# Retention and a Mish feed-forward layer on one core: state copies on one engine, one load and four scalings moved, four transposes moved

## The chip, the cores and the metric

The kernel runs on one core of a Trainium2 chip. The metric is device time in microseconds (us) of one execution, as the median of several runs. A core has five engines with a queue of instructions each, which run in the order in which they were issued: TensorE (PE in the profile: matmuls and transposes, with its weight loads as PEld), VectorE (DVE), ScalarE (ACT), GpSimd (POOL) and SyncE (SP). Transfers are issued from the queues of SyncE, ScalarE and GpSimd. The engines meet only through semaphores. In this kernel matmuls write to PSUM, a memory cut into banks, from which VectorE and ScalarE read; GpSimd works on the other on-chip memory, SBUF.

## What is computed

```python
def _attn_ref(q, k, v):                      # q, k, v: 8 batches, 8 heads, 576 positions, 64
    scores = scale * np.matmul(q, k.transpose(0, 1, 3, 2))
    gamma = 1.0 - 2.0 ** (-5.0 - np.arange(H))
    rel = pos[:, None] - pos[None, :]
    Dmat = np.where(rel >= 0, gamma[:, None, None] ** rel[None, :, :], 0.0)
    return np.matmul(scores * Dmat[None], v)

def _moe_ref(x, w_in, w_out):                # x: 4608 x 512, w_in: 512 x 2048, w_out: 2048 x 512
    h = x @ w_in
    g = h * np.tanh(log1p(exp(h)))           # Mish
    return g @ w_out
```

Inputs and the output are float32. The decay factorises: gamma^(i-j) = gamma^i * gamma^-j, so the kernel scales q by `gq` and v by `gv`, and only the diagonal blocks need a mask.

## The kernel before

**Chunks and states.** The 576 positions of a batch are cut into four chunks of 128 and one of 64; the last chunks of two neighbouring batches share one chunk of 128 rows. That gives 36 chunks: numbers 0 to 7 are the first chunks of the eight batches, and then come the others in pairs of batches (8 to 14 for batches 0 and 1, 15 to 21 for batches 2 and 3, and so on). The first chunks need no earlier state and go through functions of their own (`f_...`). Every other chunk needs the *state* of its batch, the sum of k times v over all earlier chunks. `state(upto)` adds one chunk to the running sum in a PSUM bank (`st`, one buffer; eight matmuls, L336) and copies the sum to SBUF (`ssb`) in two halves, each multiplied by a column of `diag` that is 1 for one half of the partitions and 0 for the other: ScalarE makes the first half (L339), VectorE the second (L340). Both read the same bank and the next `state` writes to it. The first term of a batch's state takes k from `k0[b]` (`load_k0`, L252, a transfer on GpSimd's queue) and v from `v0s[b]` (`f_state`, L248, a product on GpSimd).

**Steps of a chunk n.** `load(n)` issues q, k and v on GpSimd's queue (L266, L270). P: VectorE scales q (L276). V: GpSimd scales v (L282). T: eight transposes on TensorE into a buffer of the PSUM pool `sc` (two buffers) and a ScalarE copy (L291, L292) for n < 18, a transposing transfer on SyncE's queue for the others (L294). S: scores (L304) into a buffer of `sc`, and the masked copy by VectorE (L308). O: state and masked scores to the chunk's result (L354, L359) into the same buffer, and VectorE's copy to `xT` (L363).

**Tiles.** Four chunks make a tile t of 512 rows (t = 0 to 8). For a tile `g1(t, f)` computes one of 16 slices of the first projection (four matmuls, L373, then Mish on ScalarE, L375), and `g2(t, i)` a quarter of the second projection of one chunk (four matmuls, L388). After the last quarter `stores()` copies the sums by VectorE (L424) and issues the output's transfer; the copy frees the PSUM bank (`ops` with one buffer, or `hp` with two).

**Order.** The order is written out by hand, and each engine's queue follows it. After the first stage (chunks 0 to 7) comes a loop over 24 steps u = 4j + w (L511 to L540) in which tile 1 is projected while chunks 8 to 13 are prepared. In it GpSimd's queue gets, at w = 0 of j = 1 to 4: V of chunk 8 + j, `f_state(1, j - 1)` (batches 4 to 7) and `load(11 + j)`, and at j = 5: V of chunk 13, the loads of chunks 16 and 17, `load_k0(2)` and `load_k0(3)`. The state of batch 2 begins in the next loop, at t = 2, i = 4. That loop (L543 to L577) runs over t = 2 to 9 and 16 steps i, where w = i % 8: scores stand at w = 0, outputs at w = 4, with up to one state at w = 0 and two at w = 4 (before and after the outputs). `by_pe` is true only in the tile at t = 2; there the transposes of chunks n + 2 and n + 3 stand at w = 6 and 7.

The pool `vraw` has eight buffers, which hold the values of the eight first chunks and then those of the later chunks.

Of the kernel before, what the change touches and what calls it, by code (L numbers as in the profile page):

```python
# [12 lines left out]
AX = mybir.ActivationFunctionType  # L13
OP = mybir.AluOpType
# [3 lines left out]
def kernel(  # L18
# [18 lines left out]
    nc = tc.nc  # L37
    B, H, S, D = q.shape
    assert (B, H, S, D) == (8, 8, 576, 64)
    P = 128  # L40
    NP = H // 2
# [28 lines left out]
    op = ctx.enter_context(tc.tile_pool(name="op", bufs=4))  # L70
# [25 lines left out]
    v0 = {}  # L96
# [55 lines left out]
    gv = consts.tile([P, 5, H], F32)  # L152
# [4 lines left out]
    diag = consts.tile([P, 2], F32)  # L157
# [21 lines left out]
    v0s = {}  # L179
# [61 lines left out]
                                 start=(p == 0), stop=True, skip_group_check=True)  # L241
        copy(xts[t][:, :, ts(b, P)], ot)

    def f_state(t, b):

        n = 4 * t + b
        v0s[n] = first.tile([P, H, D], BF16, name="v0s", bufs=B)
        nc.gpsimd.tensor_tensor(v0s[n], v0[n], gv[:, 0, :].unsqueeze(2).to_broadcast([P, H, D]), op=OP.mult)  # L248

    def load_k0(b):  # L250
        k0[b] = first.tile([P, H, D], BF16, name="k0", bufs=B)
        nc.gpsimd.dma_start(out=k0[b], in_=k[b, :, 0:P, :].rearrange("h p d -> p h d"))  # L252
# [3 lines left out]
    def load(n):  # L256
        if n >= n_chunks:
            return
        b, c = chunks[n]
        qr = io.tile([P, H, D], F32, name="qraw")  # L260
        vr = io.tile([P, H, D], F32, name="vraw", bufs=8)
        qks = io.tile([P, 2, H, D], BF16, name="qks", bufs=9)
        live[n] = {"q": qr, "v": vr, "qks": qks}
        for t, src in ((qr, q), (qks[:, 1], k), (vr, v)):
            if c < 4:
                nc.gpsimd.dma_start(  # L266
                    out=t, in_=src[b, :, ds(P * c, P), :].rearrange("h p d -> p h d"))
            else:
                for e in range(2):
                    nc.gpsimd.dma_start(  # L270
                        out=t[ds(64 * e, 64)],
                        in_=src[b + e, :, ds(512, 64), :].rearrange("h p d -> p h d"))
# [49 lines left out]
    def state(upto):  # L322

        if upto >= n_chunks or done[0] > state_of[upto]:
            return False
        b, c = states[done[0]]
        done[0] += 1
        if c == 0:
            ks, vs = k0[b], v0s[b]
            st_ps[b] = ps_st.tile([P, NP, 64], F32, name="st")  # L330
        else:
            ks, vs = live[index[b, c]]["qks"][:, 1], live[index[b, c]]["vs"]
        st = st_ps[b]
        for p in range(NP):
            for e in range(2):
                nc.tensor.matmul(st[ds(64 * e, 64), p, :], lhsT=ks[:, 2 * p + e, :], rhs=vs[:, 2 * p + e, :],  # L336
                                 start=(c == 0 and p == 0), stop=True, skip_group_check=True)
        ssb = tr.tile([P, 2, NP, 64], BF16, name="ssb", bufs=6)
        nc.scalar.activation(ssb[:, 0], st, AX.Copy, scale=diag[:, 0:1])  # L339
        nc.vector.tensor_scalar(ssb[:, 1], st, diag[:, 1:2], None, op0=OP.mult)  # L340
        st_sb[b, c] = ssb
        return True

# [24 lines left out]
    def g1(t, f):  # L368
        if f == 0:
            gts[t] = gp.tile([P, nF, NCH * P], BF16, name="gT")  # L370
        hp = ps_h.tile([P, NCH * P], F32, name="hp")
        for c in range(KC):
            nc.tensor.matmul(hp, lhsT=w_in_t[:, c, ts(f, P)], rhs=xts[t][:, c, :],  # L373
                             start=(c == 0), stop=(c == KC - 1))
        nc.scalar.activation(gts[t][:, f, :], hp, AX.Mish)  # L375

    def g2(t, i):
        s, part = divmod(i, 4)
        if t == nT - 1:
            s = (s + 3) % 4  # L380
        if part == 0:
            if (t == nT - 1 and s % 2) or (t == 1 and s < 2):
                outs[t] = ps_h.tile([P, d_model], F32, name="hp")
            else:
                outs[t] = ps_o.tile([P, d_model], F32, name="ops")
        ops = outs[t]
        for f in range(4 * part, 4 * part + 4):
            nc.tensor.matmul(ops, lhsT=gts[t][:, f, ts(s, P)], rhs=w_out_t[:, f, :],  # L388
                             start=(f == 0), stop=(f == nF - 1))
        if part == 3:  # L390
            ready.append((t, s, ops))
# [3 lines left out]
    def stores():  # L395
        while ready:
            store(*ready.pop(), nc.vector.tensor_copy)
# [24 lines left out]
    def store(t, s, ops, copy):  # L422
        ot = op.tile([P, d_model], F32, name="res")
        copy(ot, ops)  # L424
        b, c = chunks[NCH * t + s]
        if c < 4:
            nc.sync.dma_start(out=out[ds(b * S + P * c, P), :], in_=ot)
        else:
            for e in range(2):
                nc.sync.dma_start(out=out[ds((b + e) * S + 512, 64), :], in_=ot[ds(64 * e, 64), :])  # L430

    def att(n, steps):
        if n >= n_chunks:
            return
        for step in steps:
            {"P": step_p, "V": step_v, "T": step_t, "S": step_s, "O": step_o}[step](n)
# [10 lines left out]
    for step in "T0 W2 S0 W1 T1 T2 S1 T3 S2 S3".split():  # L447
        n = int(step[1])
# [23 lines left out]
    for b in range(4):  # L472
        f_state(0, b)
        load(N0 + b)
# [9 lines left out]
    for i in range(nF):  # L484
        for step in steps.get(i, "").split():
            n = int(step[1])
# [15 lines left out]
    def more_loads(upto):  # L502
        for _ in range(2):
            if queued[0] <= upto:
                load(queued[0])
                queued[0] += 1
# [4 lines left out]
    for u in range(24):  # L511
        j, w = divmod(u, 4)
        if w == 0 and j > 0:
            att(N0 + j, "PV")
            if j < 5:
                f_state(1, j - 1)
                load(N0 + j + 3)
            else:
                more_loads(N0 + j + PF)
                load_k0(2)  # L520
                load_k0(3)
        elif w == 1 and j > 0:
            if j > 3:
                state(N0 + j - 1)
            if j < 5:
                att(N0 + j - 1, "S")
            if j < 4:
                state(N0 + j - 1)
            if j > 1:
                att(N0 + j - 2, "O")  # L530
            if j == 4:
                state(N0 + j - 1)
            stores()
        elif (w == 3 and j < 5) or (w == 2 and j == 5):
            att(N0 + j, "T")
        stores()
        if u < nF:
            g1(1, u)
        else:
            g2(1, u - nF)  # L540


    for t in range(2, nT + 1):  # L543
        for i in range(nF):
            n, w = NCH * (t + 1) + i // 8 * 2, i % 8
            if t in (3, 4) and i in (4, 12):
                load_k0(2 * t - 2 + i // 8)
            by_pe = n + 2 < NPE
            if w == 0:
                state(n + 1)  # L550
                stores()
                att(n, "S")
                att(n + 1, "S")
            if w == 4:
                state(n + 3)
                stores()
                att(n, "O")
                att(n + 1, "O")
                state(n + 3)
            if by_pe and w in (1, 3):  # L560
                att(n + 2 + w // 2, "P")
            if w in (0, 1):
                att(n + 2 + w, "V")
                more_loads(n + 2 + w + PF)
            if w - (6 if by_pe else 0) in (0, 1):
                att(n + 2 + w % 2, "T")
            if w == 7 and n + 4 >= NPE:
                att(n + 4, "P")
                att(n + 5, "P")
            stores()  # L570
            if t < nT:
                g1(t, i)
            if t == 2:
                if i % 2:
                    g2(1, 8 + i // 2)
            elif t < nT or i < 12:
                g2(t - 1, i)  # L577
# [32 lines left out]
```

## Time and profile before

| | |
|---|---|
| median of 3 runs | 326.68 us (324.84 to 327.05) |
| profiled execution | 327.7 us, of it 326.0 us span |
| TensorE busy | 304.8 us (93% of the span) |
| VectorE, ScalarE, GpSimd busy | 126.5, 128.4, 142.9 us |
| mean granted TensorE clock | 0.99 |
| two halves of the state copy, each x32 | ScalarE 473 ns, VectorE 480 ns |
| `f_state` on GpSimd, x8 | 1053 to 1530 ns, median 1090 |
| q scaling on VectorE (L276), x28 | 678 to 1416 ns, median 684 |
| `load_k0`, x8, from issue to landing | 7.4 to 16.3 us, median 8.8 |

The page gives busy times and groups of instructions with a mean duration of one; the answers of the trace give instructions in order of time (start, duration, engine, line, operation, output <- inputs, with the idle time of the engine before and what ended it in square brackets), and sums of waits (total, number, longest). In the page's rows of 40 digits each digit is a slice of the span and gives a busy share in tenths, or the clock that TensorE was granted.

### The profile page before, as it was taken

What the parts mean: (1) busy time and instruction counts of PE and PEld (TensorE: products, weight loads), DVE (VectorE), ACT (ScalarE), POOL (GpSimd) and SP (SyncE); (2) the same over time, 40 slices, a digit from 0 to 9 for tenths busy, and PEclk for the clock granted to TensorE, in tenths of its full rate; (3) what the DMA queues carried; (4) which work ended last, traced back from release to release, by engine and by line L of the source; (5) the groups of instructions that cost most, each with busy time, mean ns of one, the idle gap of its engine ahead of it and who ended that gap; (6) DMA issues with size and microseconds to landing.
All of it is one profiled execution on the core that took longest, in us unless ns stands there. A gap on an engine that the chain in (4) does not pass through costs nothing.

```text
span 326.0 us, 5926 instructions
## 1 busy us (share of the span) xinstructions
PE 304.8 (93%) x2439; PEld 151.6 (46%) x2478; DVE 126.5 (39%) x195; ACT 128.4 (39%) x223; POOL 142.9 (44%) x174
## 2 busy tenths in 40 slices
PE   5889999999939999999999999999999999999995
PEld 2543445555415545444544444545454444444444
DVE  2722555655623634443434443434344332000111
ACT  4666237773415453342424333333343332333200
POOL 5572359999992894819280808062010000000000
PEclk9999999999969999999999999999999999999999
DMA  7999999977999599999999969981322300010031
GB/s 177 214 205 244 238 223 258 216 126 149 208 188 151 91 199 135 227 126 167 141 182 114 194 112 169 123 161 53 60 68 56 77 32 34 32 32 32 34 96 65
DMA packets 79850, 44.10 MB, mean 135 GB/s; under 512 B 63056, under 2 KB 71504, under 8 KB 79824
## 3 DMA queue, kind: packets, MB, share of 16 engines
q0 software_dynamic: 47376, 24.98, 53.3%
q1 hardware_dynamic: 31872, 18.23, 26.1%
q10 hardware_dynamic: 576, 0.52, 0.6%
q8 instruction: 19, 0.31, 0.4%
q14 instruction: 7, 0.06, 0.1%
HBM read 38.80 MB, written 9.44 MB: 148 GB/s over the span
## 4 chain that ended last, share of the span: by engine, by line
PE 71%; DMA 11%; POOL 7%; issue 4%; DVE 3%; ACT 2%; SPq 1%; ACTq 0%; DVEq 0%; POOLq 0%
PE hp L373 29%; PE ops L388 25%; PE hp L388 4%; DMA w_in_t<-in_moe_w_in_dram 4%; DMA k<-in_k_dram 2%; PE hp L405 2%; PE st L336 2%; POOL vs L282 2%; DMA vraw<-in_v_dram 2%; ACT ssb L339 2%; DMA gT<-in_k_dram 2%; DMA qks<-in_k_dram 2%; PE sc L304 1%; POOL qraw L266 1%; DVE ssb L340 1%
## 5 line engine op out<-in xcount | busy, mean ns | idle before, releaser
L373 PE MATMUL hp<-xT,w_in_t 128*128 128x512 bf16 x548 | 142.4, 383 | 3.0 <-DVE gq L475 0.8
L375 ACT ACTIVATE gT<-hp 128x512 bf16<-128x512 f32 x144 | 86.1, 598 | 129.3 <-PE hp L373 117.3
L388 PE MATMUL ops<-w_out_t,gT 128*128 128x512 bf16 x429 | 110.0, 379 | 1.0 <-DVE res L424 0.5
L373 PEld LDWEIGHTS <-w_in_t 128*128 128x128 bf16 x576 | 53.9, 98 | 64.7 <-DMA w_in_t<-in_moe_w_in_dram 2.4
L388 PEld LDWEIGHTS <-gT 128*128 128x128 bf16 x496 | 48.3, 98 | 59.4 <-issue 2.8
L424 DVE COPY res<-ops 128x512 f32<-128x512 f32 x28 | 19.2, 687 | 75.2 <-PE ops L388 74.9
L340 DVE TENSOR_SCALAR ssb<-st,diag 128x256 bf16<-128x256 f32 x32 | 15.4, 480 | 75.4 <-ACT ssb L339 75.4
L266 POOL DMA_DIRECT2D qraw<-in_q_dram x24 | 22.5, 938 | 39.9 <-DVE qks L276 36.9
L282 POOL TENSOR_TENSOR vs<-vraw,gv 128x512 bf16<-128x512 f32 x28 | 30.2, 1087 | 20.8 <-issue 14.2
L308 DVE TENSOR_TENSOR sm<-sc,mask 128x1024 bf16<-128x1024 f32 x28 | 33.0, 1216 | 6.0 <-PE sc L304 6.0
L339 ACT ACTIVATE ssb<-st,diag 128x256 bf16<-128x256 f32 x32 | 15.1, 473 | 26.5 <-PE st L336 26.5
L266 POOL DMA_DIRECT2D vraw<-in_v_dram x24 | 21.9, 911 | 2.3 <-DMA w_out_t<-in_moe_w_out_dram 2.0
L266 POOL DMA_DIRECT2D qks<-in_k_dram x24 | 21.7, 906 | 2.4 <-DMA w_out_t<-in_moe_w_out_dram 2.4
L276 DVE TENSOR_TENSOR qks<-qraw,gq 128x512 bf16<-128x512 f32 x28 | 21.7, 806 | 1.2 <-DMA qraw<-in_q_dram 1.2
L363 DVE CAST xT<-sc 128x512 bf16<-128x512 f32 x24 | 15.3, 681 | 0.0
L388 PE MATMUL hp<-w_out_t,gT 128*128 128x512 bf16 x61 | 14.6, 379 | 0.3 <-issue 0.2
L270 POOL DMA_DIRECT2D qraw<-in_q_dram x8 | 5.6, 708 | 15.7 <-DVE qks L276 15.7
L292 ACT COPY qkT<-sc 128x1024 bf16<-128x1024 bf16 x10 | 10.1, 1012 | 4.7 <-PE sc L291 4.7
L248 POOL TENSOR_TENSOR v0s<-vraw,gv 128x512 bf16<-128x512 f32 x8 | 9.9, 1240 | 0.0
L354 PE MATMUL sc<-qkT,ssb 128*64 128x128 bf16 (+1 forms) x224 | 9.5, 213 | 0.0
L336 PEld LDWEIGHTS <-qks 128*64 128x64 bf16 x192 | 5.1, 110 | 9.3 <-issue 7.6
L359 PE MATMUL sc<-sm,vs 128*64 128x128 bf16 x192 | 9.4, 219 | 0.0
(93 smaller groups left out, 202.5 us busy)
## 6 DMA issues: line engine op xcount, KB each, us to landing
out_dram<-res SPq DMA_DIRECT2D x31, 256.0 KB, 2.3
vraw<-in_v_dram POOLq DMA_DIRECT2D x28, 256.0 KB, 6.8
qraw<-in_q_dram POOLq DMA_DIRECT2D x24, 256.0 KB, 5.1
qks<-in_k_dram POOLq DMA_DIRECT2D x24, 128.0 KB, 5.7
w_in_t<-in_moe_w_in_dram POOLq DMA_DIRECT2D x4, 512.0 KB, 8.4
w_out_t<-in_moe_w_out_dram POOLq DMA_DIRECT2D x4, 512.0 KB, 22.3
gT<-in_q_dram SPq DMA_DIRECT2D x15, 128.0 KB, 6.1
gT<-in_k_dram SPq DMA_DIRECT2D x9, 128.0 KB, 9.0
```

The source lines that it names most:

```text
L266: nc.gpsimd.dma_start(out=t, in_=src[b, :, ds(P * c, P), :].rearrange("h p d -> p h d"))
L276: nc.vector.tensor_tensor(live[n]["qks"][:, 0], live[n]["q"], gq[:, c, :].unsqueeze(2).to_broadcast([P, H, D]), op=OP.mult)
L282: nc.gpsimd.tensor_tensor(vs, live[n]["v"], gv[:, c, :].unsqueeze(2).to_broadcast([P, H, D]), op=OP.mult)
L308: nc.vector.tensor_tensor(sm.rearrange("p e n i -> p (e n) i"), sc.rearrange("p e n i -> p (e n) i"), m.unsqueeze(1).to_broadcast([P, 2 * ...
L336: nc.tensor.matmul(st[ds(64 * e, 64), p, :], lhsT=ks[:, 2 * p + e, :], rhs=vs[:, 2 * p + e, :], start=(c == 0 and p == 0), stop=True, skip ...
L339: nc.scalar.activation(ssb[:, 0], st, AX.Copy, scale=diag[:, 0:1])
L340: nc.vector.tensor_scalar(ssb[:, 1], st, diag[:, 1:2], None, op0=OP.mult)
L363: nc.vector.tensor_copy(xts[t][:, :, ts(s, P)], ot)
L373: nc.tensor.matmul(hp, lhsT=w_in_t[:, c, ts(f, P)], rhs=xts[t][:, c, :], start=(c == 0), stop=(c == KC - 1))
L375: nc.scalar.activation(gts[t][:, f, :], hp, AX.Mish)
L388: nc.tensor.matmul(ops, lhsT=gts[t][:, f, ts(s, P)], rhs=w_out_t[:, f, :], start=(f == 0), stop=(f == nF - 1))
L424: copy(ot, ops)
```

## The change

The state copy becomes one VectorE instruction: `st` is read twice by a repeated dimension and multiplied by the two columns of `diag`, repeated along the row. `f_state` takes its engine as an argument; the calls for batches 4 to 7 now go to VectorE, and stand at w = 2 instead of w = 0. `load_k0(2)` moves from j = 5 (behind the loads of chunks 16 and 17) to j = 4 (ahead of the load of chunk 15). In the main loop the stores at w = 0 go ahead of the state, and TensorE's transposes at t = 2 move from w = 6 and 7 to w = 5 and 6.

```diff
-    def f_state(t, b):
+    def f_state(t, b, engine=nc.gpsimd):
 
         n = 4 * t + b
         v0s[n] = first.tile([P, H, D], BF16, name="v0s", bufs=B)
-        nc.gpsimd.tensor_tensor(v0s[n], v0[n], gv[:, 0, :].unsqueeze(2).to_broadcast([P, H, D]), op=OP.mult)
+        engine.tensor_tensor(v0s[n], v0[n], gv[:, 0, :].unsqueeze(2).to_broadcast([P, H, D]), op=OP.mult)
...
         ssb = tr.tile([P, 2, NP, 64], BF16, name="ssb", bufs=6)
-        nc.scalar.activation(ssb[:, 0], st, AX.Copy, scale=diag[:, 0:1])
-        nc.vector.tensor_scalar(ssb[:, 1], st, diag[:, 1:2], None, op0=OP.mult)
+        nc.vector.tensor_tensor(
+            ssb.rearrange("p e n d -> p e (n d)"),
+            st.rearrange("p n d -> p (n d)").unsqueeze(1).to_broadcast([P, 2, NP * 64]),
+            diag.unsqueeze(2).to_broadcast([P, 2, NP * 64]), op=OP.mult)
...
         if w == 0 and j > 0:
             att(N0 + j, "PV")
             if j < 5:
-                f_state(1, j - 1)
+                if j == 4:
+                    load_k0(2)
                 load(N0 + j + 3)
             else:
                 more_loads(N0 + j + PF)
-                load_k0(2)
                 load_k0(3)
...
             stores()
+        elif w == 2 and 0 < j < 5:
+            f_state(1, j - 1, nc.vector)
         elif (w == 3 and j < 5) or (w == 2 and j == 5):
             att(N0 + j, "T")
...
             if w == 0:
+                stores()
                 state(n + 1)
-                stores()
                 att(n, "S")
                 att(n + 1, "S")
...
-            if w - (6 if by_pe else 0) in (0, 1):
-                att(n + 2 + w % 2, "T")
+            if w - (5 if by_pe else 0) in (0, 1):
+                att(n + 2 + (w == 1 or w == 6), "T")
```

## The prediction

> **What bounds the kernel now.** I read the page's busy times and clock row first, then TensorE's waits by length, then the stretch with the longest of them in order of time, then one steady tile in order of time.
>
> On the page, in 40 slices of 8.15 us:
>
> ```profile
> PE   5889999999939999999999999999999999999995
> PEclk9999999999969999999999999999999999999999
> ```
>
> TensorE is the bound: 304.8 us busy of a span of 326.0. Nothing off it counts unless TensorE waits for it. One slice stands out, the 12th, with a third of the work, and the granted clock falls in it. The waits of TensorE:
>
> ```profile
> PE st L336 <- DMA k<-in_k_dram: 5.6, 2, 5.3
> ...
> PE st L336 <- DVE ssb L340: 2.3, 10, 0.3
> ```
>
> The first is one wait of 5.3 us (the second of its two is 0.3, at 142.67, of the same length and in the same place as the ssb waits, so I count it with them). In order of time, around it:
>
> ```profile
> 87.27 1.82 POOL L252 DMA_DIRECT2D k<-in_k_dram  x2
> ...
> 89.08 0.39 PE L359 MATMUL sc<-sm,vs 128*64 128x128 bf16 x8
> ...
> 94.77 0.43 PE L336 MATMUL st<-v0s,k 128*64 128x64 bf16 x8 [5.30 <-DMA k<-in_k_dram]
> ```
>
> Batch 2's k is issued at 87.27 and lands 7.4 us later, while TensorE wants it at 89.4. GpSimd issues it late because its queue has no gap from 49.5 to 100. A steady tile in order of time, with both kinds of small wait (start, duration, engine, line):
>
> ```profile
> 183.28 1.04 PE L373 MATMUL hp<-xT,w_in_t 128*128 128x512 bf16 x3
> ...
> 183.74 0.68 DVE L424 COPY res<-ops 128x512 f32<-128x512 f32 x1
> ...
> 184.48 1.02 PE L388 MATMUL ops<-w_out_t,gT 128*128 128x512 bf16 x4 [0.16 <-DVE res L424]
> ...
> 190.61 0.32 PE L336 MATMUL st<-vs,qks 128*64 128x64 bf16 x8
> ...
> 190.97 0.47 ACT L339 ACTIVATE ssb<-st,diag 128x256 bf16<-128x256 f32 x1 [0.52 <-PE st L336]
> ...
> 191.48 0.48 DVE L340 TENSOR_SCALAR ssb<-st,diag 128x256 bf16<-128x256 f32 x1 [4.79 <-ACT ssb L339]
> ...
> 192.11 0.32 PE L336 MATMUL st<-vs,qks 128*64 128x64 bf16 x8 [0.28 <-DVE ssb L340]
> ```
>
> The two halves of the state copy run one after the other, and the second state's matmuls wait for both because they write the bank that is being read. At 184.48 the second projection waits for the output copy, which was queued behind the state copy.
>
> **Part 1: k of batch 2 sooner, four scalings off GpSimd.** The four v0s products at L248 hold GpSimd's queue 1.48 + 1.47 + 1.47 + 0.99 = 5.4 us (start to next start at 60.34, 65.52, 70.69, 77.29). Without the first three, the scaling of chunk 12's v ends at 77.29 - 4.42 = 72.9, and k is issued there: 14.4 us sooner. L252's transfers took 7.4 to 16.3 us to land (median 8.8), so it lands at about 81.7, at worst 89.2. TensorE wants it at 89.4, less some 0.6 that parts 2 and 3 save before it (0.25 at 73.76, 0.34 at 83.85): 88.8. Cover 7.1 us; at the worst landing 0.4 us would remain. k is moved past chunk 15's three loads and those of chunks 16 and 17; chunk 15's are put back by 0.9 us (one issue) but are 4.4 sooner by the scalings, the others run 5.4 sooner.
>
> What the hole costs is read against the next block of the same kind, at i = 12 of this tile. There the second state starts 1.50 us after the first (108.89 to 110.39), so here it would have at 88.26 + 1.50 = 89.76 instead of 94.77: 5.0 us. From that state to the next scores it takes 6.43 us there (to 116.82) and 8.29 here (to 103.06): 1.9 us, the lower clock (granted 0.50 in 92 to 96, 0.66 in 96 to 100). **Gain 6.9 us.** What is late next: the following inputs are values of chunk 15 (wanted by the state at 108.89, in the new time near 101.5, and scaled at 95.36 - 5.4 = 90.0) and q of chunk 18 (loading once chunk 13's q is freed). GpSimd then waits for freed q buffers again, as it does at 107.01 now (6.88 us), so TensorE sets its pace.
>
> The v0s products on VectorE: the same form at L276 takes 0.68 alone and 1.21 to 1.42 beside GpSimd products (59.76, 64.87, 69.90). VectorE idles 1.77, 1.63 and 1.91 us in each pass of this stage (before 62.74, 67.77, 73.22). It gets 0.7 to 1.5 more, and 0.2 for the longer copy. Queued behind it is the next chunk's q scaling, which ended at 66.14 for transposes at 70.09: 4 us of room. I take nothing; if the cover is gone, each pass is late by 0.1. The Trainium skill (GPSIMD Engine Reference, Specifications) says that GpSimd shares its SBUF interfaces with VectorE and collides with instructions that have two SBUF inputs, which speaks against this move; its rule would put every one of the four at the contended price, 4 x 0.74 = 3.0 us more VectorE time in all, still under the idle time. One new wait: loads of chunks 12 to 15 may take over the value buffers that these products read. GpSimd reaches the values of 13, 14, 15 near 65.8, 70.5, 75.5 and the products end near 65.8, 70.8, 76.4: up to 0.9 us of GpSimd's queue (with the next k and loads behind it), inside the 7.1.
>
> **Part 2: the state copy in one instruction.** No row shows this form. Nearest: L363, 512 elements from PSUM, 0.68; L308, a product with a broadcast from PSUM, 1.22 for 1024, which at L363's slope gives the same 0.68. Upper end: twice L340's 0.48, 0.96. I take 0.68, by the row of equal size. From the first state's start it is ready after 0.36 (190.61 to 190.97) + 0.68 + about 0.12 (191.96 to 192.11, and 0.06 at 73.76) = 1.16; TensorE is ready itself after 1.05 to 1.1 (the same outputs without a state, 272.59 to 273.64: 1.05). Second states now start 1.40 (five) or 1.50 (six) after the first: 11 x 1.45 - 11 x 1.16 = 3.2, and 0.3 for the one in the hole, less 0.1 for rounding: **3.4 us**. At 0.96 the sum is 1.44 and the gain 0.1. The Trainium skill (VectorE: DVE Perf Modes, the perf-mode tier table) gives a product no more than one element a cycle from PSUM and a single-source operation up to two, against merging the copies; by its formula of (N + 151) cycles at 0.96 GHz a 512-element product would be an estimated 0.69 us, which leaves the gain at 3.3. ScalarE loses 15.1 us of copies; TensorE never waits for it in the steady tiles, so nothing.
>
> **Part 3: the output copy before the state copy.** It matters only where a state stands at w = 0: 83.85, 135.04, 184.48, 250.14. Four matmuls at 0.216 from 183.28 end at 184.14; the next start at 184.48: 0.34 lost, the same at the others. Put first, the copy starts when its sums are done (182.4) and ends at 183.1. The state copy waits up to 0.7 for it, with scores' masks behind, needed only four steps later (6 us). **Gain 4 x 0.34 = 1.4 us.**
>
> **Part 4: transposes a step sooner.** Only in the tile at t = 2, four of them. They write score buffers that the xT copies free: at 0.36 + 0.68 + 0.62 = 1.7 us after the first state, against transposes at 1.1 + 0.24 + 0.86 = 2.2 (outputs, second state, one projection slice): no wait, 0.5 to spare. They may free ScalarE before the scores: scores to first projection take 0.78 at 103.06 and 116.82 against 0.55 at 149.93. Bounds +0.5 and -0.5; I take 0.
>
> **Sum.** 6.9 + 3.4 + 1.4 = 11.7 us. The profiled execution took 327.7 (span 326.0, 1.7 around it), 1.0 above the median 326.68. Profiled 316.0, span 314.3; median **315.0 us**.
>
> **Rivals.** A: the hole goes, but the copy costs 0.96 and the transposes nothing: 6.9 + 1.4 = 8.3, 318.4 us. For it: an unseen form. Against: two rows at 0.68. B: another input takes the hole's place (a transfer that lands 16 us late, a buffer wait) and half of it stays, 3.4 of 6.9: 318.4 with part 2, 321.6 without. Against: GpSimd is 5 us ahead everywhere. C: the change moves k, but TensorE's stop hangs on something else issued in the same place, and only small gains come: about 323.5, no difference. Against: it restarts 7.4 us after this issue, the shortest landing of L252. D, slower: the product with two broadcast operands is slow out of PSUM, in the twelve places where a second state waits. The present chain equals a product of 0.99; to eat the 8.3 us of the other parts it must take 0.99 + 8.3 / 12 = 1.68 us, and 2.0 gives about 330.5. For it: both operands repeat elements, which no PSUM row does. Against: the longest PSUM row is 1.22, for twice the columns.
>
> **How the numbers follow.** A measurement can tell about 1% from no change, here 323.4 and 329.9. Chances: forecast 0.60 (313 to 317.5, by the landing and 0.5 of part 4), A 0.17, B 0.10, C 0.07, D 0.06. Faster: forecast, A and B, 0.87; same C, 0.07; slower D, 0.06. The range 312.5 to 320.5 takes in the forecast, A and a part of B.
>
> **What would show it.** The 12th slice at 9 in both rows; no wait of L336 for k over 0.5; one VectorE copy of about 0.68 with 32 of it and no L339; second states 1.15 after first; no wait for L424 at w = 0. Wrong if a wait over 2 us stands between 80 and 110, if the copy takes over 1 us, or if VectorE's lateness shows as TensorE waits between 60 and 80.

## The result and the profile after

The changed kernel takes 314.94 us in the median (314.66 to 315.26, four runs) against 325.76 (322.56 to 327.05, four runs) before: a ratio of 0.968 with a 95% interval of 0.961 to 0.976. The forecast was 315.0. The profiled execution took 315.04 us, 313.3 of it span, against 327.7 and 326.0. An execution more than 1.5% above the fastest of its kernel counts as slow and is left out of the medians and ratios here.

The same two rows of the page, TensorE's busy tenths and its granted clock in 40 slices of 7.83 us:

```profile
PE   5889999999999999999999999999999999999995
PEclk9999999999999999999999999999999999999999
```

The slice with a third of the work is gone, and so is the lower clock. The longest of TensorE's waits in the changed kernel, by total, number and longest (L375, L390 and L426 are now the lines of the first projection, the second projection and the output copy):

```profile
PE hp L200 <- DVE qb L188: 2.6, 1, 2.6
PE ops L174 <- DVE lnd L129: 1.3, 1, 1.3
PE hp L375 <- DMA w_in_t<-in_moe_w_in_dram: 0.8, 1, 0.8
```

None is for k, for a state copy or for an output copy; what is left stands before 20 us, apart from three of 0.2. The place of the hole, in order of time:

```profile
72.62 0.93 POOL L252 DMA_DIRECT2D k<-in_k_dram  x1
...
86.84 0.32 PE L336 MATMUL st<-vs,qks 128*64 128x64 bf16 x8
...
87.94 0.32 PE L336 MATMUL st<-v0s,k 128*64 128x64 bf16 x8
...
94.37 0.62 PE L304 MATMUL sc<-qkT 64*128 64x128 bf16 x16
```

Batch 2's k is issued at 72.62 instead of 87.27 and landed 3.9 us later, 11.4 us ahead of its use. The second state follows the first after 1.10 us, where it took 6.51, and the next scores follow that state after 6.43, where they took 8.29. The steady tile, at the same steps as the one shown of before:

```profile
171.97 0.32 PE L336 MATMUL st<-v0s,k 128*64 128x64 bf16 x8
172.08 0.69 DVE L426 COPY res<-ops 128x512 f32<-128x512 f32 x1 [3.92 <-PE ops L390]
...
172.69 0.68 DVE L339 TENSOR_TENSOR ssb<-st,diag 128x512 bf16<-128x512 f32 x1
172.77 1.04 PE L375 MATMUL hp<-xT,w_in_t 128*128 128x512 bf16 x3
...
173.64 1.03 PE L390 MATMUL ops<-w_out_t,gT 128*128 128x512 bf16 x4
```

The output copy now goes ahead of the state copy (172.69) and ends at 172.77, so the second projection follows the first without a gap. The new state copy takes 674 to 693 ns (median 683, 32 of them).

Where the 12.7 us between the two spans come from, read as distances between the same instructions in both traces:

| stretch | before | after | difference |
|---|---|---|---|
| start to the first scores of the main part | 57.72 | 56.93 | 0.79 |
| first to second state, batch 2 (t = 2, i = 4) | 6.51 | 1.10 | 5.41 |
| that state to the next scores | 8.29 | 6.43 | 1.86 |
| first to second state, eleven other places | 1.40 or 1.50 | 1.10 or 1.20 | 3.3 |
| a state at w = 0 to the next state, four places | 8.13 to 8.14 (6.41 at t = 2) | 7.81 (6.08) | 1.30 |
| scores at i = 8, t = 2, to the state at i = 12 (transposes) | 5.84 | 5.84 | 0.0 |

The change makes 11.9 of it. The 0.8 at the start is not counted: three profiles of the changed kernel have their first scores at 56.9, 60.9 and 60.3 us, so the start varies by more than that by itself (see the last section).

### The profile page after: what moved, and what is told of

Read it like the earlier page. It is cut to its first block, busy times and chain, and to the rows that moved or that the text cites. A ratio compares the mean times of both kernels' runs of the same rounds, so it can differ in the third digit from the quotient of the medians.

```text
span 313.3 us, 5883 instructions
## 1 busy us (share of the span) xinstructions
PE 301.2 (96%) x2439; PEld 150.9 (48%) x2478; DVE 136.0 (43%) x199; ACT 113.4 (36%) x191; POOL 138.5 (44%) x170
## 4 chain that ended last, share of the span: by engine, by line
PE 92%; DMA 5%; issue 1%; ACTq 0%; POOL 0%; SPq 0%; DVE 0%; POOLq 0%
PE hp L375 40%; PE ops L390 30%; PE hp L390 4%; PE sc L304 3%; PE st L336 3%; PE hp L407 2%; DMA w_in_t<-in_moe_w_in_dram 2%; PE sc L356 2%; PE sc L361 2%; DMA gT<-in_k_dram 2%; DMA vraw<-in_v_dram 1%; PE sc L291 1%; PE st L407 1%; PE hp L418 1%; PE ops L407 1%
## 5 line engine op out<-in xcount | busy, mean ns | idle before, releaser
L375 PE MATMUL hp<-xT,w_in_t 128*128 128x512 bf16 x548 | 140.9, 380 | 2.0 <-DMA w_in_t<-in_moe_w_in_dram 0.8
L390 PE MATMUL ops<-w_out_t,gT 128*128 128x512 bf16 x429 | 109.9, 379 | 0.5
L375 PEld LDWEIGHTS <-w_in_t 128*128 128x128 bf16 x576 | 53.6, 98 | 62.7 <-DMA w_in_t<-in_moe_w_in_dram 1.4
L390 PEld LDWEIGHTS <-gT 128*128 128x128 bf16 x496 | 48.2, 98 | 58.1 <-issue 0.8
L426 DVE COPY res<-ops 128x512 f32<-128x512 f32 x28 | 19.3, 688 | 83.2 <-PE ops L390 79.6
L339 DVE TENSOR_TENSOR ssb<-st,diag 128x512 bf16<-128x512 f32 x32 | 21.9, 685 | 46.8 <-PE st L336 46.8
L365 DVE CAST xT<-sc 128x512 bf16<-128x512 f32 x24 | 15.4, 682 | 0.0
L390 PE MATMUL hp<-w_out_t,gT 128*128 128x512 bf16 x61 | 14.6, 379 | 0.3 <-issue 0.2
L270 POOL DMA_DIRECT2D qraw<-in_q_dram x8 | 5.6, 710 | 11.7 <-DVE qks L276 11.7
L304 PE MATMUL sc<-qkT 64*128 64x128 bf16 x224 | 9.0, 218 | 0.0
L252 POOL DMA_DIRECT2D k<-in_k_dram x8 | 7.4, 920 | 3.2 <-DMA w_out_t<-in_moe_w_out_dram 3.2
L304 PEld LDWEIGHTS <-qkT 64*128 64x128 bf16 x224 | 6.3, 94 | 4.9 <-issue 3.4
```

Source lines behind the costliest of these rows:

```text
L304: nc.tensor.matmul(sc[:, e, p, :], lhsT=qk[r, 1, p, :], rhs=qk[r, 0, p, :], start=True, stop=True)
L339: nc.vector.tensor_tensor(ssb.rearrange("p e n d -> p e (n d)"), st.rearrange("p n d -> p (n d)").unsqueeze(1).to_broadcast([P, 2, NP * 64 ...
```

## The experiments

Each was made from the changed kernel. Because the start varies by some microseconds from run to run, the safer measure is the distance from the first scores of the main part (the first L304) to the start of the last ones: 207.3 us before, 195.4 after. Times of runs stand beside it.

**The changed kernel again.** No edit.

> The changed kernel unaltered, as the measure for the others on this chip. Both theories: 315 us, with no wait of TensorE for k or for a state copy after 60 us.

316.85 us (314.67 to 319.25). First to last scores 195.7; 0.2 more than in the first profile, all of it at the second state of 76.87 us, which starts 1.34 after the first instead of 1.10. That is a late state copy, though the sums of waits don't name it: VectorE starts the copy at 76.14 instead of 75.89, because the moved scaling at 73.28 took 1.48 here and the q scaling behind it 1.52; the copy ends at 76.82. So the expectation of no wait for a state copy missed by 0.2 us. TensorE waits 3.9 us for the weights of the first projection, until 20.7 us, and not at all for k.

**Batch 2's k back behind the loads of chunks 16 and 17.**

```diff
-                if j == 4:
-                    load_k0(2)
                 load(N0 + j + 3)
             else:
                 more_loads(N0 + j + PF)
+                load_k0(2)
                 load_k0(3)
```

> Only the load of batch 2's k goes back behind the loads of chunks 16 and 17; the scalings stay on VectorE. Theory (the wait is set by when GpSimd's queue reaches this issue, and both edits move that): the issue comes at about 82.1 us (where the changed kernel has 83.14 for batch 3's k, one issue of 0.9 to 1.1 sooner), lands 7.4 to 8.9 us later, at 89.5 to 91.0, against 87.9 where TensorE wants it: a wait of 1.6 to 3.1 us and little clock loss, 316.6 to 318.5 us. Rival 1 (the scalings were what mattered, the place of the load does nothing): 315 us, no wait. Rival 2 (the place of the load is everything, the relief of GpSimd is worth nothing): the whole hole of 5.0 us and 1.9 of lower clock, 322 us.

317.2 us (316.62 to 320.79), and no wait for k. In order of time:

```profile
81.08 1.82 POOL L252 DMA_DIRECT2D k<-in_k_dram  x2
...
88.75 0.32 PE L336 MATMUL st<-v0s,k 128*64 128x64 bf16 x8
```

The first of the two transfers landed 5.4 us after its issue, at 86.5, where I had put 7.4 to 8.9: 2.3 us ahead of its use. The expectation missed by the landing time, and by nearly 2 us of issue time (82.1 on the clock of a run whose start was 0.8 sooner). So the relief of GpSimd alone closes the hole, and rival 1 fits this run; but the next one shows that it isn't the relief as such. The profile had one new wait, 1.7 us at 126.9 for a transposing transfer (first to last scores 197.3). A second look at the same kernel:

> The kernel with only batch 2's k put back, a second time, to see whether TensorE's wait of 1.7 us for a transposing transfer near 125 us belongs to it. If it does: a wait for that transfer over 1 us again, and 197.3 us from the first scores to the last. If it was chance: no such wait, 195.4 us. In either case no wait for k, as k is issued at about 81 us and wanted at 88.

316.66 us (316.53 to 317.07) against 316.46 of the changed kernel on the same chip; no wait for k, none for a transposing transfer, first to last scores 195.4. Here k landed 6.4 us after its issue and only 0.8 ahead of its use, so the relief of GpSimd by itself closes the hole with little to spare. The wait did not come again, so as far as one repeat can tell it does not belong to the edit. It still shows what may stand next in line: the first four of those transfers landed 8.2 to 11.4 us after their issue in the changed kernel and 10.4 to 15.0 in the run that waited, with scores asking at about the same time.

**The four scalings back on GpSimd, k left in its new place.**

```diff
             if j < 5:
+                f_state(1, j - 1)
                 if j == 4:
                     load_k0(2)
...
-        elif w == 2 and 0 < j < 5:
-            f_state(1, j - 1, nc.vector)
```

> Only the four scalings of batches 4 to 7 go back to GpSimd at w = 0; the load of batch 2's k stays in its new place. Theory: k is issued at about 77.5 us (72.6 + 1.48 + 1.47 + 1.47, and 0.99 less the last), lands at 85 to 86.5 against 87.9: no wait, 315 us within 0.5. Rival (GpSimd's relief carries the gain): k comes after 87.9 and TensorE waits 1 us or more, 316 us or more. Second rival (VectorE's longer list costs TensorE time): below 314.5 us.

315.38 us (314.95 to 316.17); first to last scores 195.4, the same as changed. k was issued at 77.46, as expected, and landed after 3.4 us. The place of the load alone closes the hole too.

**Both back.** The two diffs above together.

> Both go back; state copy, stores and transposes stay as changed. Theory: the issue comes where it came before, less 0.8 us of an earlier start, at 86.5; it lands 7.4 us later at 93.9, against 87.9: a wait of 6.0 us, longer than the 5.0 of before because TensorE now reaches the place 0.6 sooner and asks 0.35 sooner, and 1.9 us or more of lower clock: 322.9 us. Rival (the hole is worth the 6.9 us of the prediction whatever stands around it): 321.9 us. Rival (the wait was a coincidence of that profile): under 318 us.

322.82 us (319.69 to 323.22). In order of time:

```profile
86.94 1.82 POOL L252 DMA_DIRECT2D k<-in_k_dram  x2
87.40 0.32 PE L336 MATMUL st<-vs,qks 128*64 128x64 bf16 x8
...
93.66 0.43 PE L336 MATMUL st<-v0s,k 128*64 128x64 bf16 x8 [5.05 <-DMA k<-in_k_dram]
...
102.52 0.62 PE L304 MATMUL sc<-qkT 64*128 64x128 bf16 x16
```

The hole is back: 6.26 us from first to second state instead of 1.10, and 8.86 instead of 6.43 to the next scores: 5.2 + 2.4 = 7.6 us, as the distance from first to last scores says (203.0 against 195.4). The wait is 5.2 and not the expected 6.0 because the transfer landed after 6.7 us instead of 7.4, and the clock took 2.4 instead of 1.9. The granted clock in two stretches of 4 us behind the wait, this kernel (busy time of each engine, then clock, DMA share and GB/s):

```profile
92.00:96.00 4.00, 2.12 (x14) 1.17 (x16) 0.69 (x1) 0.05 (x1) 4.00 (x5) 0.50 1.43 198
96.00:100.00 4.00, 4.00 (x25) 2.20 (x23) 0.00 (x0) 2.15 (x3) 3.82 (x5) 0.65 1.34 193
```

TensorE is full from 96 to 100 and still slow: that part of the loss is the clock (0.50 and 0.65), and a busy share doesn't show it.

**The state copy back in two halves.**

```diff
-        nc.vector.tensor_tensor(
-            ssb.rearrange("p e n d -> p e (n d)"),
...
+        nc.scalar.activation(ssb[:, 0], st, AX.Copy, scale=diag[:, 0:1])
+        nc.vector.tensor_scalar(ssb[:, 1], st, diag[:, 1:2], None, op0=OP.mult)
```

> Only the state copy goes back to two halves, on ScalarE and VectorE; the rest as changed. Theory (the chain of two copies holds the bank against the second state's matmuls in twelve places): second states again 1.40 to 1.50 us after the first instead of 1.10 to 1.20, 12 x 0.30 = 3.6 us, 318.6 us. Rival (TensorE's small waits were slack that other waits would take): under 316 us. Rival (ScalarE, with 15 us more, holds Mish back too): over 320 us.

320.63 us (318.69 to 322.8); first to last scores 199.05, 3.6 more than changed. The second states are at 1.40 or 1.50 again, and TensorE's waits for the copy are back:

```profile
PE st L336 <- DVE ssb L340: 2.5, 11, 0.3
```

The listed idle time, 2.5 us in eleven places and 0.3 in the twelfth, which is put down to a transfer, is less than the 3.6 that the copies cost (the ends of matmuls are modelled), so distances between starts are the safer measure.

**State ahead of the stores.**

```diff
-                stores()
                 state(n + 1)
+                stores()
```

> Only the order at w = 0 goes back: state first, then stores. Theory: the output copy now follows one copy of 0.68 instead of a chain of 1.0, so it ends 0.36 + 0.60 + 0.68 = 1.64 us after the state's start, and TensorE wants the bank after 1.66: a loss of 0 to 0.1 in each of four places, 315.0 to 315.4 us. Rival (the prediction's sum, in which this part is worth 1.4 us by itself): four waits of 0.34, 316.4 us.

316.01 us (314.77 to 317.89); first to last scores 195.54, 0.1 more than changed. At the step shown above, where the state's matmuls start at 171.63:

```profile
172.60 0.68 DVE L426 COPY res<-ops 128x512 f32<-128x512 f32 x1
...
173.33 1.02 PE L390 MATMUL ops<-w_out_t,gT 128*128 128x512 bf16 x4
```

The output copy ends at 173.28. TensorE has finished the first projection's slice at 173.29 (172.43 and four matmuls of 0.216) and goes on at 173.33. The order of the stores is worth almost nothing behind the single copy.

**Both: two halves, and state ahead of the stores.**

> The state copy in two halves and the state ahead of the stores. Theory: 3.6 us as with the two halves alone, and now the full 4 x 0.34 = 1.4 us as well, because the output copy waits for the longer chain: 320.0 us; the stores' order is worth 1.4 with two halves and nearly nothing with one. Rival (the parts add): the sum of what the two show alone, 318.6 with 0 to 0.4 more.

321.61 us (319.61 to 323.82); first to last scores 200.34, 4.9 more than changed. Behind the longer chain the order costs 4.90 - 3.61 = 1.29. The parts do not add.

**Transposes back at w = 6 and 7.**

```diff
-            if w - (5 if by_pe else 0) in (0, 1):
-                att(n + 2 + (w == 1 or w == 6), "T")
+            if w - (6 if by_pe else 0) in (0, 1):
+                att(n + 2 + w % 2, "T")
```

> Only the transposes of the tile at t = 2 go back to w = 6 and 7. Theory (nothing waits for them in either place): 315.0 us within 0.2. Rival (ScalarE's copies of 1.0 us stand ahead of Mish just before the scores, 0.22 us in each of two places): 315.5 us and a gap of 0.78 from scores to the first projection. Rival (they take a free score buffer too soon now): 314.5 us.

316.66 us (315.89 to 318.84); first to last scores 195.44, the same to 0.01 us. Nothing waits for them in either place.

**The state copy issued twice.**

```diff
+        for _ in range(2):
-        nc.vector.tensor_tensor(
+            nc.vector.tensor_tensor(
...
```

> The changed kernel with the state copy issued twice, so that it costs 1.28 us in a row instead of 0.68. Theory (the copy has no slack in front of the second states, and only there): second states 0.36 + 1.28 + 0.12 = 1.76 us after the first instead of 1.10 to 1.20, 12 x 0.60 = 7.3 us: 202.7 us from the first scores to the last. Rival (VectorE has slack everywhere, the 3.6 us came from ScalarE's part): under 197 us. Rival (VectorE becomes the bound, in the stage between 55 and 80 us above all): over 205 us.

326.34 us (325.65 to 329.37), no better than before the change (ratio 1.005, interval 1.001 to 1.009); first to last scores 207.96, 12.5 more than changed. From 90 us on the second states come 1.92 us after the first (1.83 once). That makes 8.4 of it in eleven places, more than the 0.60 in each that were expected, since the pair takes 1.40, the second copy starting 0.72 after the first. Another 0.6 stands near 131 us, where scores waited 0.4 for a transposing transfer. The other 3.6 arise between 72 and 81 us, where VectorE turned into the bound:

```profile
71.72 1.89 DVE L276 TENSOR_TENSOR qks<-qraw,gq 128x512 bf16<-128x512 f32 x1
...
73.53 1.40 DVE L340 TENSOR_TENSOR ssb<-st,diag 128x512 bf16<-128x512 f32 x2
...
75.08 0.32 PE L336 MATMUL st<-v0s,k 128*64 128x64 bf16 x8 [1.78 <-DVE ssb L340]
```

The first state's matmuls start at 72.09. The scaling of q comes late here and is lengthened, from its usual 0.68, to 1.89; the copy waits behind it on VectorE's queue, TensorE behind the copy. The second state comes 2.99 us after the first instead of 1.10, which is 1.9 of the 3.6. The other 1.7 are the clock once more: it was granted at 0.50 from 75.6 to 79.0 us, with TensorE busy all the time, and the next state came 5.93 us later instead of 4.25.

**A try to go further: the first weights in two loads.**

```diff
-    load_w_in(0, 512)
+    load_w_in(0, 256)
+    load_w_in(256, 256)
```

> The changed kernel, with the first load of the first projection's weights (512 columns) issued as two of 256. Theory (the spread of the runs and the last long wait of TensorE come from this load): half the bytes land first, the wait of 0.8 to 3.9 us near 18 us goes to 0.5 or less, TensorE's clock stays up behind it, and the median falls by 1 to 2.5 us against the control with less spread. Rival (the 16 DMA engines are full there, so smaller pieces land no sooner, and rows of half the length cost more): the same or up to 1 us slower, the wait moved to the second half.

with, on the same chip,

> The changed kernel unaltered on this chip. Every theory: 314.5 to 319 us, according to how long TensorE waits for the first projection weights near 18 us (0.8 us in one profile, 3.9 in another); 195.4 us from the first scores to the last.

317.17 us (316.48 to 318.28) against 316.46 (315.83 to 318.96): no gain. The wait of 2.6 in the control becomes several, 3.0 in all, in the split kernel:

```profile
PE hp L375 <- DMA w_in_t<-in_moe_w_in_dram: 3.0, 3, 1.9
```

The first piece lands in time and later ones do not. This fits the rival, that transfers fill this stretch: from 16 to 28 us the DMA share (the packets' times, which overlap, over the time of 16 engines) is 1.18 to 1.25 here and 1.17 to 1.19 in the control. That this is the reason was not tested by itself. None of the versions tried is better than the changed kernel.

## Why the prediction was right

**The hole.** Put at 5.0 us of wait and 1.9 of clock; measured 5.0 to 5.1 (5.41 less the 0.3 to 0.4 that the single state copy brings in this place) and 1.86. The comparison with the next block of the same kind was the step that found the clock's share, which no wait shows. The issue was put at 72.9 and came at 72.62. The landing was put at 8.8, the median over the whole run, which was too long for this stage; it was 3.9, and in this stage the same transfer landed after 3.4 to 7.5 us in all the profiles. This erred on the safe side here, and the cover was 11.4 us instead of 7.1; in the experiment with k put back the same habit made me forecast a wait that did not come.

**Two edits, one gain.** The prediction counted the move of k and the relief of GpSimd as one part. The experiments show that each of them alone is enough, at 195.4 us from first to last scores; only with both undone is the time lost. Rival C, that TensorE's stop hung on something else, falls with that run: the wait for k came back with the issue at 86.94.

**The state copy.** Put at 0.68 from the row of equal size, measured 0.683; second states put at 1.16 on average, measured 1.10 and 1.20; 3.4 us forecast, 3.6 found by undoing it. Rival A's 0.96 is refuted. Rival D did not come, but its price was too low. It took a longer copy as a matter of twelve places, by which a copy of 1.40 would cost 12 x (1.40 - 0.68) = 8.6 us; the pair that takes 1.40 cost 12.5, of which 3.6 lay in the early stage, 1.9 as a wait and 1.7 as lower clock. VectorE's idle time in a pass of that stage is 0.6 to 1.3 us in the changed kernel (before 61.95, 66.98 and 71.93). A pair of 1.40 brings the kernel back to where it began, so the break-even of 1.68 worked out for rival D was too far off. (Rival B's time without part 2 should have been 321.8 by its own terms, not 321.6.)

**The stores.** Put at 1.4, found to be 1.3 between the two traces. But this is its worth behind the two halves; behind the single copy it is 0.1. The single copy, in turn, is worth 3.6 with the output copy first and 200.34 - 195.54 = 4.8 with the state first, since it also shortens the output copy's wait. The sum was right because the prediction counted that shared part once, under the stores: 3.4 + 1.4 = 4.8, where undoing both cost 4.9.

**The transposes.** Put at nothing, and nothing it was. The bound of 0.5 came from 0.78 us between scores and projection at 103.06 and 116.82. The stretch from these scores on is equally long in both kernels (5.84 us), so nothing was lost there: the group at 103.84 has records of seven matmuls where there were eight weight loads, so what looked like a wait of 0.16 was most likely a missing first record.

**The scalings on VectorE.** Put at nothing, with 0.7 to 1.5 us each: they took 0.68 three times and 1.10 once, and the q scalings behind two of them 1.53. The undone version is equally fast (195.4), so the cover held in this profile; in the first control it failed by the 0.2 us told above, which is the lateness of 0.1 in a pass that the prediction allowed for, somewhat larger and in one pass. Of the buffer wait of up to 0.9 that was feared on GpSimd's queue nothing is seen but two gaps of 0.17 (before 70.92 and 73.72), for which the profile names no releaser.

**The median.** The 1.0 us by which the profiled run lay above the median was carried over; for the changed kernel it was 0.1. This and the 0.8 us of a shorter start nearly cancelled in the profile's account, so the agreement of 315.0 with 314.94 is closer than the working deserves. In two later groups of runs the changed kernel has medians of 316.85 and 316.46, against 326.45 and 325.13 before: ratios of 0.971 (0.965 to 0.978) and 0.975 (0.970 to 0.981). So the gain of a whole execution lies between 8.7 and 10.8 us by the medians, less than the 11.7 forecast for it, while the part behind the start gained 11.9.

## What to carry to other kernels

When the busiest engine is idle once for long, compare the stretch behind the wait with a later block of the same kind: the time after restarting is part of the price. Read how late an input is from its place in the issuing queue, and take the landing time from transfers issued under the same load, not from the median, and note how far it spreads (3.4 to 7.5 us here). Two edits to one wait are not two gains, and a reordering whose worth rests on a slow instruction ahead of it loses that worth when the instruction becomes fast; undo edits one by one and in pairs before giving each a number.

## What the runs showed of the hardware

**The start varies.** The first scores of the main part stand at 56.5 to 60.9 us in the profiles of these kernels, whose code up to there is the same but for the split load, and most of it is TensorE's wait for the first weights near 18 us, 0.8 to 3.9 us, with the lower clock that followed some of these waits. This is of the size of the spread of the changed kernel's runs (314.66 to 319.25); unprofiled runs can't be split, so that it is the whole reason is not shown.

**The clock.** Behind a wait of TensorE the granted clock either stayed at 1.00 or fell to 0.50 for a spell of 3.4 us (20.7 to 24.1 in the first control, 75.6 to 79.0 with the copy doubled) or 6.8 us (91.9 to 98.7 in the kernel before). The length of the wait alone does not decide it. After the weights' wait the clock was 1.00 from 20 to 24 us where the wait was 0.85 (first profile of the changed kernel), 1.8 (second look with k put back) or 2.8 (two halves with the state ahead of the stores); with 2.6 it was 0.50 (control of the last group, and two halves alone), with 3.9 it was 0.59 (first control). The Trainium skill (TensorE: Matmul & The Clock Gate, Part 1) says that a free-running window of about 3.4 us decides, idle ones halving the clock. The spells of one and two times 3.4 us agree with that figure, and a window that runs by itself would explain why 2.8 us passed once without a loss. But the stretch need not be wholly idle: in the 3.4 us before the clock fell at 75.6, TensorE was busy for 1.6. How much work keeps the clock up, the runs don't show.

**Doubled work costs more than its duration.** Two state copies in a row took 1.40 us, 0.72 from start to start, while two copies that write different parts of xT (L365) take 1.28 together: 0.60 from start to start. That the shared output is the reason was not tested alone.
